# Startup mask, clock fillers and last copy of a block-sparse attention with a gated MLP behind it: one-hots by Pool selects, band by VectorE, row-tile fillers, split copy

## The chip, the cores and the metric

The kernel runs on one core of a Trainium2 chip. The metric is the device time of one execution in microseconds (us), given as the median over runs. Engines are named as in the profile: PE is TensorE (PEld its weight loads), DVE is VectorE, ACT is ScalarE, POOL is GpSimd, SP is the engine that issues most DMAs.

## The reference

For 4 batches, 8 heads, 768 tokens and head size 64, the reference computes attention with a block mask (blocks of 32 tokens, 24 x 24 blocks), and then a gated MLP on the 512 concatenated columns.

```python
scores = (1/8) * q @ k.T                      # per batch and head, 768 x 768
mask  = |block_i - block_j| <= 1              # band
mask |= block_i in (0, 23) or block_j in (0, 23)
mask |= block_j in sampled_blocks[block_i]    # 3 random blocks per row
x = softmax(where(mask, scores, -1e9)) @ v    # heads side by side: 4 x 768 x 512

h = relu(x @ w_in)                            # 512 -> 1024
u, v = h[..., :512], h[..., 512:]
v = (v - mean(v)) / sqrt(var(v) + 1e-6)       # per token
v = w_spatial @ v + b_spatial[:, None]        # over the 768 tokens
out = (u * v) @ w_out                         # 4 x 768 x 512, float32
```

## The kernel before

The mask is added inside the score matmul. Each head's transposed k (`kt`) and q (`qt`) tiles have 88 partitions: 64 of head data and 24 mask rows. In `kt`, mask row b holds a one at the tokens of block b (the block one-hots). In `qt`, the mask rows hold, per query token, 0 for an allowed block and -300 for a forbidden one; they come from one small matmul pair `mq` (L252) of the 24 x 24 block mask `bm` with the one-hots. So the score matmuls L289 (two of 384 columns per 128 keys) give masked scores, and ScalarE's exponential (L293, scale 0.125) follows. `av` (L305) multiplies by v, with a ones column that gives the softmax sums; `norm` divides.

The order is written out by hand and each engine executes its own list in program order; the recording layer adds the semaphore waits. The main loop goes over 16 head pairs in 12 steps each. A step issues one score chunk, some preparation of the next pairs, `av` of seven steps earlier, and a share of the MLP of the previous batch. The MLP of the last batch runs after the loop, as the tail.

The startup, in program order, is what the change touches:

- SP and ACT issue the loads of `sampled_blocks` (`samp_i`), k, q and v.
- VectorE writes zeros into `warm`, `allowed`, `ind_nat` and `tiny` (L170 to L173); ScalarE loads its function table and runs an exponential on `tiny`.
- TensorE gets `keep_warm(8, 512)` (L183): eight matmuls of 512 columns on zeros, whose result `wps` nobody reads. They keep TensorE active until data arrive.
- Pool makes `colidx`, five selects on `allowed` (band and border rows, L190 and L193), one select on `ind_nat` (L195, the one-hots in natural token order), `ident` (the identity for transposes), the ones column of `vv`, and `mhalf`.
- VectorE sets the border columns of `allowed`, casts `samp_i` to `samp_f` (L207), adds the sampled blocks in three steps (L209), forms `bm` (L213) and casts the first q head `nat_q` (L109). ScalarE casts the first k head `nat_k` (L107) and copies `ind_nat` into `ind` in the chunked token order (L217).
- `tr_head` (L225): six transposes of k on TensorE (L228) and a VectorE copy into `kt[0]` (L220); a VectorE copy of `ind` into the mask rows (L248); two fillers; the `mq` pair; a ScalarE copy of `mq` into `qt[0]` (L223); six transposes of q and their copy; six fillers; then the loop.

In the tail, 24 matmul units take their PSUM bank from `moe_ps`, which goes round the tags `sc`, `av` and `moe` (two buffers each) in `tail_tags`. The tag `moe` is also used by the transposes `xtr` just before the tail and by `g_tr` in it. Each output chunk is copied from PSUM to `osb` alternately by ScalarE (L447) and VectorE (L449) and stored by a DMA (L450).

```python
        tail_tags.rotate(1)                       # L355: moe, av, sc, moe, ...
```

The softmax here doesn't subtract the row's maximum and nothing guards it: scores larger than these inputs give would overflow.

## Time and profile before

| | |
|---|---|
| median of 7 runs | 227.0 us (226.46 to 228.18) |
| profiled execution | 227.45 us |
| its span | 225.5 us, 5286 instructions |
| busy | PE 214.6 (95%), ACT 171.1 (76%), DVE 131.1 (58%), POOL 64.1 (28%) |
| first filler matmul, first score matmul, first exponential | 1.17, 7.66, 8.19 us |
| last VectorE copy | 221.81 us, 0.69 us long |

The span is the time from the first to the last instruction on the core. A busy TensorE counts matmuls from their issue to their modelled end, so matmuls that overlap in the pipeline are counted once and a busy TensorE need not be at its peak. In a timeline line the columns are start, length, engine, source line, operation, tile written <- tiles read, shapes, count; in brackets stands the idle time in front and what ended it. In the chain of waits the columns are start, length, and the work or wait.

### The profile page before, as it was taken

To read this page: it belongs to the slowest core of one execution; us is meant where nothing else is said; L and a number is where in the kernel's file an instruction comes from. 1 tells how busy PE (TensorE), PEld (TensorE's weight loads), DVE (VectorE), ACT (ScalarE), POOL (GpSimd) and SP (SyncE) were. 2 spreads that over 40 slices of the span, in tenths; PEclk is the share of its full clock that TensorE was granted. 3 is DMA by queue.
4 is the path that set the end of the run, shared out by engine and by line. 5 is a ranking of instruction groups with operands and counts; after the bars stand their busy time and mean duration, and the time that the engine had idled before them with its cause. 6 is when DMAs were issued, how large, how long until landed. Compare 5 with 4: busy or idle time off the path is not lost.

```text
span 225.5 us, 5286 instructions
## 1 busy us (share of the span) xinstructions
PE 214.6 (95%) x2119; PEld 130.7 (58%) x2148; DVE 131.1 (58%) x282; ACT 171.1 (76%) x245; POOL 64.1 (28%) x88
## 2 busy tenths in 40 slices
PE   7899999999999999999999999999999999999993
PEld 3467777766665555666656555666565555544551
DVE  5556445368993444379993534469983323675532
ACT  5699999997799676878898677877898666266351
POOL 5535770349493401210283101211240000012000
PEclk9999999999999999999999999999999999999999
DMA  6689979996996974999465565987050424610016
GB/s 203 216 291 380 384 270 317 373 116 78 268 252 123 287 102 124 224 349 283 169 110 207 107 97 157 285 282 200 0 105 3 81 49 83 230 52 0 0 50 234
DMA packets 56093, 40.27 MB, mean 179 GB/s; under 512 B 39300, under 2 KB 51588, under 8 KB 56068
## 3 DMA queue, kind: packets, MB, share of 16 engines
q1 hardware_dynamic: 55780, 39.53, 65.6%
q10 hardware_dynamic: 288, 0.39, 0.5%
q8 instruction: 17, 0.28, 0.5%
q14 instruction: 8, 0.07, 0.1%
HBM read 24.38 MB, written 6.29 MB: 136 GB/s over the span
## 4 chain that ended last, share of the span: by engine, by line
PE 74%; ACT 19%; DMA 2%; issue 2%; DVE 1%; ACTq 0%
PE ps L289 21%; ACT a_all L293 19%; PE ps_av L305 10%; PE ps_moe L424 10%; PE ps_moe L402 7%; PE ps_moe L379 7%; PE ps_moe L442 5%; PE ps_t L424 2%; DMA out_dram<-osb 2%; PE wps L180 2%; PE ps_t L379 2%; PE ps_t L442 2%; PE ps_t L402 1%; PE ps_sc L424 1%; PE ps L228 1%
## 5 line engine op out<-in xcount | busy, mean ns | idle before, releaser
L293 ACT ACTIVATE a_all<-ps 128x768 bf16<-128x768 f32 x192 | 143.0, 812 | 29.9 <-PE ps L289 29.6
L289 PE MATMUL ps<-qt,kt 88*128 88x384 bf16 x384 | 93.5, 324 | 4.1 <-ACT a_all L293 2.8
L305 PEld LDWEIGHTS <-a_all 128*128 128x128 bf16 x1152 | 60.3, 98 | 28.5
L305 PE MATMUL ps_av<-vv,a_all 128*128 128x65 bf16 x1152 | 67.6, 194 | 0.0
L289 PEld LDWEIGHTS <-kt 88*128 88x128 bf16 x384 | 28.9, 97 | 8.2 <-issue 5.2
L427 DVE SCALAR_TENSOR_TENSOR gn<-ps_moe,b_col,un 128x512 bf16<-128x512 f32 x18 | 13.5, 751 | 27.3 <-PE ps_moe L424 27.3
L112 POOL CAST vv<-st_v 128x768 bf16<-128x768 f32 x16 | 13.4, 839 | 51.7 <-PE ps_av L305 46.9
L424 PE MATMUL ps_moe<-vn,w_spt 128*128 128x512 bf16 x99 | 24.8, 378 | 0.5
L424 PEld LDWEIGHTS <-w_spt 128*128 128x128 bf16 x144 | 13.8, 97 | 14.3
L392 POOL TENSOR_SCALAR std<-mv 128x3 f32<-128x3 f32 x8 | 1.9, 242 | 65.2 <-DVE mv L389 53.9
L109 POOL CAST nat_k<-st_k 128x768 bf16<-128x768 f32 x15 | 12.5, 833 | 21.5 <-DMA st_k<-in_k_dram 9.2
L319 DVE TENSOR_TENSOR xn<-ps_av,rc 128x384 bf16<-128x384 f32 x32 | 17.8, 557 | 1.1
L442 PE MATMUL ps_moe<-w_out_t,gt 128*128 128x512 bf16 x66 | 18.2, 378 | 0.3
L379 PE MATMUL ps_moe<-w_in_t,xt 128*128 128x512 bf16 x66 | 18.0, 378 | 0.3
L402 PE MATMUL ps_moe<-w_in_t,xt 128*128 128x512 bf16 x66 | 17.7, 378 | 0.3
L388 DVE BATCH_NORM_STATS2 stats<-vsb 128x6 f32<-128x512 bf16 x24 | 16.7, 694 | 1.9 <-ACT vsb L383 1.3
L379 PEld LDWEIGHTS <-xt 128*128 128x128 bf16 x96 | 9.3, 96 | 10.0 <-issue 0.7
L449 DVE COPY osb<-ps_moe 128x512 f32<-128x512 f32 x9 | 6.2, 691 | 15.0 <-PE ps_moe L442 14.9
L402 PEld LDWEIGHTS <-xt 128*128 128x128 bf16 x96 | 9.3, 96 | 9.6
L442 PEld LDWEIGHTS <-gt 128*128 128x128 bf16 x96 | 8.9, 97 | 8.4
L385 DVE TENSOR_SCALAR vsb<-ps_moe 128x512 bf16<-128x512 f32 x18 | 12.3, 681 | 1.5 <-PE ps_moe L379 1.4
L318 DVE RECIPROCAL rc<-ps_av 128x6 f32<-128x6 f32 x32 | 6.0, 187 | 12.2 <-PE ps_av L305 12.1
(82 smaller groups left out, 200.2 us busy)
## 6 DMA issues: line engine op xcount, KB each, us to landing
st_v<-in_v_dram SPq DMA_DIRECT2D x16, 384.0 KB, 5.4
out_dram<-osb SPq DMA_DIRECT2D x24, 256.0 KB, 2.5
st_q<-in_q_dram SPq DMA_DIRECT2D x15, 384.0 KB, 3.9
st_k<-in_k_dram SPq DMA_DIRECT2D x15, 384.0 KB, 4.8
wst<-in_moe_w_spatial_dram SPq DMA_DIRECT2D x3, 768.0 KB, 8.9
wst<-in_moe_w_in_dram SPq DMA_DIRECT2D x4, 512.0 KB, 9.3
wst<-in_moe_w_out_dram SPq DMA_DIRECT2D x2, 512.0 KB, 6.7
st_k<-in_k_dram ACTq DMA_DIRECT2D x2, 192.0 KB, 2.9
```

Source lines behind the costliest of these rows:

```text
L109: eng.tensor_copy(out=dst, in_=src)
L112: nc.gpsimd.tensor_copy(out=vv[p % 3][:, :, :, 0:D], in_=st.pop(("v", p)).rearrange("p h (c d) -> p h c d", d=D))
L289: nc.tensor.matmul(out=ps[:, hf * 512:hf * 512 + HALF], lhsT=kt[j % 4][:, ci * 128:(ci + 1) * 128], rhs=qt[j % 4][:, hf * HALF:(hf + 1) * ...
L293: nc.scalar.activation(out=a_ref[j][:, ci, :].rearrange("p (b c) -> p b c", b=2), in_=ps.rearrange("p (b c) -> p b c", b=2)[:, :, 0:HALF], ...
L305: nc.tensor.matmul(out=av_ref[j][:, qc, :], lhsT=a_ref[j][:, ci, qc * 128:(qc + 1) * 128], rhs=vv[p % 3][:, h, ci, :], start=(ci == 0), st ...
L319: nc.vector.tensor_tensor(out=xn_ref[p][:, :, h, :], in0=ps[:, :, 0:D], in1=rc.to_broadcast([128, NCH, D]), op=ALU.mult)
L379: nc.tensor.matmul(out=ps, lhsT=xt(g)[:, tcc * 128:(tcc + 1) * 128], rhs=w_in_t[:, g, DH:DFF], start=(g == 0), stop=(g == NDM - 1))
L388: nc.vector.bn_stats(out=stats, in_=vsb[:, tcc, :])
L402: nc.tensor.matmul(out=ps, lhsT=xt(g)[:, tcc * 128:(tcc + 1) * 128], rhs=w_in_t[:, g, 0:DH], start=(g == 0), stop=(g == NDM - 1))
L424: nc.tensor.matmul(out=ps, lhsT=w_spt[:, sc, tcc * 128:(tcc + 1) * 128], rhs=vn[:, sc, :], start=(sc == 0), stop=(sc == NCH - 1))
L427: nc.vector.scalar_tensor_tensor(out=gn[:, tcc, :], in0=ps, scalar=b_col[:, tcc:tcc + 1], in1=un[:, tcc, :], op0=ALU.add, op1=ALU.mult)
L442: nc.tensor.matmul(out=ps, lhsT=gt[:, tcc, dhc, :], rhs=w_out_t[:, dhc, :], start=(dhc == 0), stop=(dhc == NDH - 1))
```

## The change

Four parts.

1. *Mask rows in place.* `ind` is now the mask rows of `kt[0]` itself (partitions 64 to 87) and all small mask tiles lie on the same partitions. VectorE fills the rows with ones and Pool cuts them to the one-hots with two selects in the chunked token order. The tile `ind_nat`, ScalarE's copy L217 and VectorE's copy L248 go. The `mq` pair works on partitions 64 to 87.
2. *Band by VectorE.* The five Pool selects on `allowed` go. Pool makes three index tiles, and VectorE forms border rows and band with four small steps. VectorE writes the zeros of `ident`, ScalarE casts the first q head.
3. *Fillers.* Eight fillers of 512 columns become two of 512 columns, twelve of 65 columns, and 24 of 65 columns that use 64 rows each, alternately the upper and the lower half, into two PSUM banks. The two fillers of 128 columns in front of `mq` go.
4. *Tail.* `tail_tags` goes round in the order `sc`, `moe`, `av`; the last output chunk is copied by ScalarE and VectorE, half each.

```diff
-    nc.vector.memset(warm, 0.0)
-    nc.vector.memset(allowed, 0.0)
-    nc.vector.memset(ind_nat, 0.0)
-    nc.vector.memset(tiny, 0.0)
+    ind = kt[0][D:KR, :]
+    # allowed, colidx, dist, row, samp_i, samp_f, bm, sq: tiles on partitions D to KR too
+    nc.vector.memset(tiny, 0.0)
+    nc.vector.memset(warm, 0.0)
+    nc.vector.memset(ind, 1.0)
+    nc.vector.memset(ident, 0.0)
...
-    keep_warm(8, 512)
+    keep_warm(2, 512)
+    keep_warm(12, VA)
+    for _ in range(12):
+        for half, ps in ((0, wps), (1, wps2)):
+            rows = slice(64 * half, 64 * half + 64)
+            nc.tensor.matmul(out=ps[:, 0:VA], lhsT=warm[rows, 0:128], rhs=warm[rows, 0:VA],
+                             start=True, stop=True)
...
-    nc.gpsimd.iota(colidx, ...)
-    (five affine_selects on allowed, one on ind_nat, make_identity)
+    for t, pat, base, mul in ((colidx, 1, 0, 0), (dist, 1, 0, -1), (row, 0, 1 - NB, 2)):
+        nc.gpsimd.iota(t, pattern=[[pat, NB]], base=base, channel_multiplier=mul, ...)
+    tok = ind.rearrange("b (c p) -> b c p", c=NCH)
+    nc.gpsimd.affine_select(out=tok, in_=tok, compare_op=ALU.is_ge, fill=0.0, base=0,
+                            pattern=[[1, NCH], [NCH, 128]], channel_multiplier=-BLK)
+    nc.gpsimd.affine_select(out=tok, in_=tok, compare_op=ALU.is_ge, fill=0.0, base=BLK - 1,
+                            pattern=[[-1, NCH], [-NCH, 128]], channel_multiplier=BLK)
+    nc.gpsimd.affine_select(out=ident, in_=ident, compare_op=ALU.not_equal, fill=1.0, ...)
...
+    nc.vector.scalar_tensor_tensor(out=sq, in0=row, scalar=1.0, in1=row, mult, mult)
+    nc.vector.tensor_scalar(out=allowed, in0=sq, scalar1=float((NB - 1) ** 2), is_ge)
+    nc.vector.scalar_tensor_tensor(out=sq, in0=dist, scalar=1.0, in1=dist, mult, mult)
+    nc.vector.scalar_tensor_tensor(out=allowed, in0=sq, scalar=1.0, in1=allowed, is_le, max)
...
-    cast_qk(0, "q", slice(0, 1), nc.vector)
     cast_qk(0, "k", slice(0, 1), nc.scalar)
-    nc.scalar.activation(out=ind, in_=ind_nat.rearrange("b (p c) -> b c p", c=NCH), func=AF.Copy)
+    cast_qk(0, "q", slice(0, 1), nc.scalar)
...
     tr_head(0, "k", dve_copy)
-    nc.vector.tensor_copy(out=kt[0][D:KR, :], in_=ind)
-    keep_warm(2, 128)
     (the mq pair and its copy: partitions D to KR instead of 0 to NB)
...
-    tail_tags = deque(["sc", "av", "moe"])
-        tail_tags.rotate(1)
+    tail_tags = deque(["av", "sc", "moe"])
+        tail_tags.rotate(-1)
...
-                if tcc % 2 == 0:
+                if last and tcc == NCH - 1:
+                    nc.scalar.activation(out=osb[:, 0:DM // 2], in_=ps[:, 0:DM // 2],
+                                         func=AF.Copy)
+                    nc.vector.tensor_copy(out=osb[:, DM // 2:DM], in_=ps[:, DM // 2:DM])
+                elif tcc % 2 == 0:
```

## The prediction

> **What bounds the kernel now.** I read the chain of waits first, then the start and the end as timelines, because the change touches only these two.

> ```profile
> 1.17 3.59 PE wps L180 x8
> 4.77 0.78 PE ps L228 x6
> 5.54 0.33 PE wps L180 x2
> 5.87 0.68 PE mq L252 x2
> 6.56 0.47 PE ps L228 x6
> ...
> 7.05 0.56 DVE qt L220
> ...
> 7.66 0.51 PE ps L289 x2
> ```

> This is the chain up to the first score matmul, all TensorE in program order: eight fillers, six k transposes, two fillers, the two mask matmuls `mq`, six q transposes; then one VectorE copy releases L289 at 7.66. From 12.27 the chain is ScalarE's exponentials, later TensorE, and no input load stands in it. So I take a shift of the first score matmul to reach the end in full.

> ```profile
> 2.43 0.99 POOL L195 TENSOR_SCALAR_AFFINE_SELECT ind_nat<-ind_nat 24x768 bf16<-24x768 bf16 x1
> 3.63 0.29 POOL masks.py:199 TENSOR_SCALAR_AFFINE_SELECT ident<-ident 128x128 bf16<-128x128 bf16 x1
> 2.51 1.07 DVE L207 CAST samp_f<-samp_i 24x6 f32<-24x6 int32 x1 [0.96 <-DMA samp_i<-in_sampled_blocks_dram]
> 3.62 0.33 DVE L209 SCALAR_TENSOR_TENSOR allowed<-colidx,samp_f,allowed 24x24 f32<-24x24 f32 x1
> 4.52 0.17 DVE L213 TENSOR_SCALAR bm<-allowed 24x24 bf16<-24x24 f32 x1
> ```

> Pool and VectorE in the same stretch. A cast of six columns takes 1.07 us and ends at 3.59, when Pool's select and the memset behind it are done; the L209 step that began 0.01 us before Pool's 3.63 select ended 0.03 us after it, at 3.95. The next two L209 steps, with no select beside them, take 0.23 each, 0.265 start to start. So VectorE is held through Pool's selects. `bm` is ready at 4.69, and `mq` does not wait for it: TensorE only gets there at 5.80.

> ```profile
> 4.70 0.85 PE L228 MATMUL ps<-ident,nat_k 128*64 128x128 bf16 x6
> 5.80 0.75 PE L252 MATMUL mq<-ind,bm 24*24 24x384 bf16 x2
> 6.49 0.52 PE L228 MATMUL ps<-ident,nat_q 128*64 128x128 bf16 x6
> 7.66 0.50 PE L289 MATMUL ps<-qt,kt 88*128 88x384 bf16 x2 [0.20 <-DVE qt L220]
> ```

> The same six transposes take 0.85 us at 4.70 and 0.52 at 6.49, and two 384-column matmuls 0.75 and then 0.50: TensorE runs at half speed until about 6.4 us, 5.2 us after its first filler, and in those 5.2 us it paused about 0.4 in all. After the last matmul (221.79) the granted clock stays at 1.00 until 224.80 and is 0.52 over 224.80:225.54: it follows activity with a delay of some us.

> ```profile
> 196.22 0.70 DVE osb L449
> 196.97 1.24 PE ps_t L379 x5
> ...
> 221.79 0.02 issue
> 221.81 0.69 DVE osb L449
> ```

> At the start of the tail TensorE waits until VectorE has emptied the bank that the first tail unit takes over; the span ends with one VectorE copy of 0.69 and the output transfer.

> The profiled execution took 227.45 (span 225.5 plus 1.95 around it). The median of the seven runs is 227.0, 0.45 lower, and they spread from 226.46 to 228.18. About 0.3% (0.7 us) is what a measurement can tell from no change.

> **Pool's chain.** VectorE now writes `ident` and the 24x768 ones first. Zeros went as 256 uint32 in 0.27 and 384 in 0.38, 0.83 ns each above 0.06 fixed; the built instruction has 768 elements: 0.70 if it goes one by one, 0.38 if in pairs. I take 0.70, the slope of the rows. [...] After `tiny` and `warm` the ones end at 1.08+0.70=1.78, the first select starts at 1.84 and takes 0.99 (L195's row), the second 2.90 to 3.89 (0.07 between dependent Pool steps, as at 3.563 to 3.633), the `ident` select 3.96 to 4.25. Before, `ident` was ready at 3.93. So the five small selects (0.20 each), the memset and the 1.21 us ScalarE copy of `ind` that go were not on the path, and two selects of 0.99 in place of one are.

> **VectorE's chain.** New are four 24x24 steps, each waiting for the one before, with the cast, three L209 steps and `bm` queued behind them. As in the 3.62 row, a step that starts within some hundredths of a Pool select loses: the first square ends with the first select (2.86), the next step with the second (3.91), the second square with the `ident` select (4.28). Then the fourth step (0.23, the L209 row) from 4.31 to 4.54, two memsets (0.06), the cast to about 4.67 (0.1, below the 0.17 row, with no Pool beside it), three steps from 4.70 to 5.47 (2x0.265+0.23), `bm` from 5.50 to 5.67. `mq` can start at 5.71. If nothing were held, `bm` would be there before 4 and `mq` would follow the k transposes (below); if the cast too were caught by Pool's small memsets, 5.8. Ends: 5.1 to 5.8.

> **TensorE.** Two 512-column fillers from 1.20 at 0.427 (the spacing of eight in 3.59) end at 2.05. No row shows a cold 65-column matmul; a warm av matmul of that shape starts every 0.03, and 65 columns at the fillers' 0.83 ns are 0.054: twelve take 0.65. The 24 row tiles take 0.65 if their pairs overlap, 1.3 if not, 2.6 if each costs a cold 128-column step (0.107). I take 1.3, nearest to the shape's own rows: the fillers end near 4.1 with 0.14 for the switch (the pause in front of 4.70), just before `ident`. k transposes go from about 4.35 to 5.0; then TensorE, with the two fillers removed, idles until `mq` at 5.71. Before, `mq` began at 5.80: a gain of 0.1, with the q transposes, the copies and the first scores shifting alike. The q cast moved to ScalarE (0.52 after 3.73 or the landing) is ready before 5.2 and hides behind this wait, the removed 0.35 `ind` copy was hidden behind the q transposes, the remaining copies keep their places.

> **The clock.** This is the cost that I think decides. Over the 3.5 us from the fifth filler (1.17+4x0.427=2.88) to the rise at about 6.4, TensorE paused 0.4 us (three pauses of 0.14). In the same stretch it now works 1.2 (fillers) + 0.65 (k transposes) + 0.66 (`mq`) and pauses about 1.0, or 1.7 if the row tiles overlap. The 1.7 us of unbroken work before 2.88 had not brought full speed, and 3.1 in the stretch behind did; 1.8 to 2.5 lies at the lower end between. If it is too little, the rise comes later by as long as the clock takes to react, some 3 us by the fall at the end. [...] Cost of a rise near 9.5: the q transposes take 0.33 more (0.85 against 0.52), the first scores 0.25 more (0.75 against 0.50), and one or two exponentials wait on a cold step of 0.85 (two 384-column matmuls 0.64, two fillers 0.21, at the fillers' 0.83 ns) instead of the 0.70 between exponentials (four in 2.92 from 8.19, the last 0.81 long): 0.2. Sum 0.78, less 0.1 from `mq`: +0.7.

> **The end.** The first tail unit moves from the bank that VectorE empties until 196.91 to one long free. Its first three matmuls can follow the transposes at 196.55, its fourth waits for `xt`, copied by VectorE until 197.38, and starts near 197.43 instead of 197.61: gain 0.18, after which TensorE runs without a wait on the banks. The split copy: in the built program VectorE's half waits for ScalarE's half, as both read one bank. ScalarE's 512 columns take 0.60 and 768 take 0.81, so 256 take 0.39; VectorE's 0.69 for 512 less 256 at 1.04 ns is 0.43; with 0.03 between, 0.85 against 0.69: a loss of 0.16. Together -0.02; at the ends -0.18 and +0.16.

> **The cases.** *Late clock*: 227.45+0.7-0.02 = 228.1 for the profiled run, 227.7 carried to the median. I take 228.0: in a run whose clock comes early (the fast ones) the old chain is all TensorE and shrinks, while the new one is held at 5.71 by Pool and VectorE, so such runs lose 0.3 more. For it: the idle TensorE in front of `mq`. Chance 0.50.

> *Clock in time* (not slower beyond measurement): 227.45-0.1-0.02 = 227.3, 226.9 to 227.3 at the median. It decides if 1.8 to 2.5 us of work in those 3.5 is enough. Against it: 1.7 was not. Chance 0.25.

> *VectorE free, clock no later* (faster): selects and steps interleave, `mq` follows the k transposes at 5.1, 0.7 earlier, of which 0.3 is lost again if the q transposes run cold: 227.45-0.4-0.02 = 227.0, 226.6 at the median, and 226.2 if the many small matmuls bring the clock up sooner. For it: VectorE's steps are tiny; against it: the 1.07 us cast. Chance 0.15.

> *Fillers too long* (slower, or the change not doing what it says): row tiles at 0.107 end at 5.4, the k transposes at 6.1, `mq` at 6.3: +0.5, 227.9, 227.5 at the median. Chance 0.10.

> **Numbers.** 228.0. Slower by over 0.3%: most of the first case and half of the last, 0.55. Faster: the third and a little of the second, 0.17. Within: 0.28. Low end 226.4 with most of the third case; high end 228.9, the first with the `mq` end of 5.8 (0.1), the split's 0.16 alone and a clock another 0.6 later.

> **What would show it.** Right: Pool's second 24x768 select ending near 3.9 with VectorE steps of about 1 us beside it, `bm` near 5.67, TensorE idle for 0.6 us in front of `mq`, q transposes of 0.8 instead of 0.52, the last VectorE half starting where ScalarE's half ends. Wrong: `bm` before 5, or q transposes at 0.52 and the first score matmul before 7.4, or halves side by side.

## The result and the profile after

The changed kernel takes 228.69 us (median of 12 runs, 228.08 to 229.88); the kernel before took 227.08 us beside it (31 runs, 226.46 to 228.28). The ratio is 1.007, with a 95% interval of 1.0053 to 1.0088: 1.6 us slower. Ratios, here and below, leave out runs more than 1.5% above the fastest of the same kernel. The profiled execution took 228.8 us, its span 227.1.

The chain of waits of the changed kernel, from the start (columns: start, length, work):

```profile
1.43 0.70 DVE kt L180
2.35 0.76 DVE sq L215
3.34 0.73 DVE sq L219
...
5.73 0.81 PE mq L267 x2
6.54 0.78 PE ps L245 x6
...
10.71 0.64 PE ps L304 x2
11.56 0.78 PE ps L245 x6
...
12.96 0.45 PE ps L245 x6
```

Up to 5.73 the chain is VectorE, where it was TensorE before. But `mq` (L267) starts at 5.73, 0.07 earlier than before. The loss comes behind it. Six transposes take 0.78 at 6.54 and still 0.78 at 11.56, then 0.45 at 12.96; a score pair takes 0.64 still at 10.71. TensorE runs at half speed (called cold below: 512 columns every 0.427 us in the first fillers, every 0.215 in the tail) for twice as long as before. The trace's record of the granted clock has the rise at 12.46 us; in the kernel before it stands at 6.37.

VectorE and Pool over the mask (timeline of each engine):

```profile
2.35 0.75 DVE L215 SCALAR_TENSOR_TENSOR sq<-row 24x24 f32<-24x24 f32 x1
3.13 0.17 DVE L217 TENSOR_SCALAR allowed<-sq 24x24 f32<-24x24 f32 x1
3.34 0.72 DVE L219 SCALAR_TENSOR_TENSOR sq<-dist 24x24 f32<-24x24 f32 x1
4.09 0.17 DVE L221 SCALAR_TENSOR_TENSOR allowed<-sq,allowed 24x24 f32<-24x24 f32 x1
...
5.51 0.17 DVE L231 TENSOR_SCALAR bm<-allowed 24x24 bf16<-24x24 f32 x1
```

```profile
2.20 0.86 POOL L204 TENSOR_SCALAR_AFFINE_SELECT kt<-kt 24x768 bf16<-24x768 bf16 x1 [0.97 <-DVE kt L180]
3.13 0.89 POOL L206 TENSOR_SCALAR_AFFINE_SELECT kt<-kt 24x768 bf16<-24x768 bf16 x1
4.09 0.34 POOL L208 TENSOR_SCALAR_AFFINE_SELECT ident<-ident 128x128 bf16<-128x128 bf16 x1
```

The two squares L215 and L219, 24x24 each, take 0.75 and 0.72 and end about 0.03 behind the selects beside them (3.10 behind 3.07, 4.06 behind 4.03). L217 between them takes 0.17 although a select runs beside it, and so does L221 beside the `ident` select; in the trace both start 0.001 before their select, the two squares 0.15 and 0.20 behind theirs. `bm` is ready at 5.68.

TensorE in the same stretch (its timeline):

```profile
2.90 0.84 PE L197 MATMUL wps<-warm 64*128 64x65 bf16 x24
4.48 0.80 PE L245 MATMUL ps<-ident,nat_k 128*64 128x128 bf16 x6 [0.74 <-POOL ident L208]
5.73 0.81 PE L267 MATMUL mq<-kt,bm 24*24 24x384 bf16 x2 [0.45 <-DVE bm L231]
6.47 0.85 PE L245 MATMUL ps<-ident,nat_q 128*64 128x128 bf16 x6
7.96 0.82 PE L304 MATMUL ps<-qt,kt 88*128 88x384 bf16 x2
```

The row tiles run two side by side, a pair every 0.0545 us (the two of a pair start within 0.003 of each other), and are issued in 0.65. TensorE then waits 0.74 for `ident` and 0.45 for `bm` (both counted from the modelled end of its work). Of the two rows that answer to those of before, the q transposes take 0.85 instead of 0.52, and the first score pair starts at 7.96 instead of 7.66 and takes 0.82 instead of 0.50.

How this adds up, in the start times of the exponentials against the profiled execution of before: the first is 0.63 late, the next three 0.78, 0.94 and 1.10, the fifth 1.61, and from there to the last of the 192 it stays at 1.61. Each of the three steps costs 0.155 because a cold score pair with two fillers needs 0.85 (0.64 and 0.21) where the exponentials come 0.70 apart; the fifth has the cold k transposes in front of it as well.

The end, from the chain of waits:

```profile
223.26 0.39 ACT osb L462
...
223.68 0.42 DVE osb L464
```

VectorE's half starts at 223.68, when ScalarE's half is done (223.65). Counted from the start of the last `x` transpose (L343; L328 before), the first tail matmul starts after 0.056 us (before 0.475), the fourth after 0.939 (1.120), the last of all after 24.739 (24.907), and the last copy ends after 25.996 (26.015). Up to the last copy the tail is even to 0.02.

### The profile page after: what moved, and what is told of

It is laid out like the page before. It is cut to its first block, busy times and chain, and to the rows that moved or that the text cites. A ratio compares the mean times of both kernels' runs of the same rounds, so it can differ in the third digit from the quotient of the medians.

```text
span 227.1 us, 5340 instructions
## 1 busy us (share of the span) xinstructions
PE 215.6 (95%) x2147; PEld 132.6 (58%) x2176; DVE 131.6 (58%) x284; ACT 171.2 (75%) x246; POOL 64.0 (28%) x85
## 4 chain that ended last, share of the span: by engine, by line
PE 77%; ACT 17%; DVE 3%; issue 2%
PE ps L304 23%; ACT a_all L308 17%; PE ps_av L320 11%; PE ps_moe L439 10%; PE ps_moe L394 7%; PE ps_moe L457 7%; PE ps_moe L417 7%; PE ps_t L439 2%; PE ps_t L457 2%; PE ps_t L394 2%; PE ps_t L417 1%; PE ps_sc L439 1%; PE ps L245 1%; PE ps_sc L417 1%; PE ps_sc L457 1%
## 5 line engine op out<-in xcount | busy, mean ns | idle before, releaser
L304 PE MATMUL ps<-qt,kt 88*128 88x384 bf16 x384 | 95.0, 328 | 3.5 <-ACT a_all L308 2.5
L421 DVE TENSOR_SCALAR vn<-vsb,mv,rstd 128x512 bf16<-128x512 bf16 x24 | 12.7, 564 | 0.6 <-POOL rstd L409 0.5
```

What stands on the lines that cost most here:

```text
L304: nc.tensor.matmul(out=ps[:, hf * 512:hf * 512 + HALF], lhsT=kt[j % 4][:, ci * 128:(ci + 1) * 128], rhs=qt[j % 4][:, hf * HALF:(hf + 1) * ...
L421: nc.vector.tensor_scalar(out=vn[:, tcc, :], in0=vsb[:, tcc, :], scalar1=mv[:, tcc, 0:1], scalar2=rstd[:, tcc:tcc + 1], op0=ALU.subtract, ...
```

## The experiments

Two theories stood at the outset. *Clock*: the new fillers and TensorE's pauses put off the rise of the clock, and nothing else matters. Rival, *mask chain*: the time goes where VectorE and Pool now hold back `mq`. Each ratio below is against runs of the kernel before that were made with it; their medians were 226.8 to 227.0.

**1. The changed kernel with the old fillers.** Only the fillers go back.

```diff
-    keep_warm(2, 512)
-    keep_warm(12, VA)
-    (24 row tiles)
+    keep_warm(8, 512)
...
+    keep_warm(2, 128)            # in front of mq
```

> The changed kernel with the fillers of before (eight of 512 columns, two of 128 in front of the mask matmuls); mask chain and tail stay changed. Theory clock: the k transposes start at 4.7 and mq at 5.8 as before, full speed comes at the same phases as before, so all of the loss goes: 227.1 (ratio to before 1.000, give or take 0.001). Rival mask chain: the loss lies in Pool's two long selects and VectorE's held steps, which are still there, so it stays at 228.3 to 228.7.

Measured: 227.1 (226.85 to 228.3) against 226.99, ratio 1.0009 [0.9984, 1.0033]. The chain of waits:

```profile
4.87 0.71 PE ps L238 x6
5.58 0.22 PE wps L188 x2
5.80 0.43 PE mq L261 x2
6.22 0.47 PE ps L238 x6
```

`bm` is ready at 5.68 as in the changed kernel, and `mq` follows the two fillers without a wait, by the timeline at 5.73 in both. Yet `mq` takes 0.43 and the q transposes 0.47: the clock rose at 5.38. So the loss is in the fillers; what the new mask and the tail cost together cannot be told from nothing (the interval is -0.4 to +0.7 us).

**2. The kernel before with the new fillers.** The reverse, with none in front of `mq`.

```diff
-    keep_warm(8, 512)
+    keep_warm(2, 512)
+    keep_warm(12, VA)
+    (24 row tiles)
...
-    keep_warm(2, 128)            # in front of mq
```

> The kernel before with the new fillers alone (two of 512, twelve of 65, 24 row tiles of 65, none in front of mq); mask chain and tail as before. Theory clock: the k transposes start 0.7 earlier (4.0) and mq at 4.9 to 5.0, but full speed comes one to two steps of 3.4 us later, first score matmul near 7.2, and the time is 228.0 to 228.6. Rival mask chain: without the slower mask chain the shorter fillers are a pure gain, 226.5.

Measured: seven of twelve runs lie between 226.16 and 229.05, with a median of 227.8; their ratio, 1.0023 [0.999, 1.0057], is not clear of no change. The other five (229.6 to 230.0) are not in it. The profiled execution took 228.3:

```profile
5.81 0.78 PE ps L235 x6
...
10.83 0.78 PE ps L235 x6
...
12.30 0.45 PE ps L235 x6
```

Its first exponential is 0.10 earlier than before, but the clock rises at 11.88 and from the fifth exponential on it is 0.95 late. In this execution the fillers alone put off the rise; what they cost in the median this experiment does not show.

**3. The changed kernel with the pauses filled.** Eight fillers more, 0.85 us of work.

```diff
     (24 row tiles)
+    keep_warm(5, 128)
...
+    keep_warm(3, 128)            # in front of mq
```

> The changed kernel with 0.85 us of fillers more, put where TensorE idled: five of 128 columns behind the row tiles (ending at 4.3, before the k transposes at 4.48) and three in front of mq (ending at 5.6, mq still at 5.73). Theory clock by idle time: full speed comes a step sooner in most runs, 227.3 to 227.8. Rival, that the clock follows how much of the array the matmuls use (row tiles, 64-column transposes and 24-row mq count little): not much better, 228.2 to 228.6. Rival mask chain: unchanged, 228.7.

Measured: 227.03 (226.84 to 229.3), ratio 1.0012 [0.9983, 1.0041]; seven of twelve runs lie between 226.84 and 227.09. 0.85 us more of fillers brings 1.66 us back, with `mq` still at 5.73. So the pauses, not the mask chain behind them, were the loss. The profiled execution was one of the exceptions (229.3), for a reason of its own that the chain of waits and the busy time by stretches show (in the second, per stretch: PE, PEld, DVE, ACT and POOL busy, then the granted clock):

```profile
17.47 0.84 POOL nat_k L108
```

```profile
15.00:19.20 4.20, 2.75 (x37) 1.84 (x37) 1.69 (x5) 2.79 (x5) 1.73 (x3) 0.99 0.90 282
19.20:22.50 3.30, 3.30 (x31) 2.28 (x29) 1.56 (x3) 2.42 (x3) 2.72 (x3) 0.50 1.05 397
```

Pool's cast of a later k block began at 17.47 (15.29 before), after its load, which landed at 17.32 (15.14 before), and TensorE had to wait for it. TensorE worked 2.75 of the 4.20 us from 15.00 on, and from 19.14 to 22.55 the clock was down to 0.50. This execution's rise at the start, 5.48, was early all the same.

**4. The tail order alone.** The kernel before with the new order of banks.

```diff
-    tail_tags = deque(["sc", "av", "moe"])
+    tail_tags = deque(["av", "sc", "moe"])
...
-        tail_tags.rotate(1)
+        tail_tags.rotate(-1)
```

> The kernel before with the new bank order of the tail alone, for its profile. Prediction's step: the first tail matmul follows the last transpose by 0.06 us, the fourth waits for xt, and from the last transpose to the end of the last matmul it takes 0.18 less than before (25.07 before, from 196.55 to 221.79 less the 0.17 of modelled end; 24.89 expected). Rival, that another bank becomes late further on: no gain.

One execution, 228.0. Its startup is that of before to the instruction, and still its clock rose at 9.95 and not at 6.37. Counted from the last `x` transpose, the last copy ends after 25.848 instead of 26.015: the order gains 0.167. The split copy of the changed kernel, which ends at 25.996, gives 0.148 of that back.

**5 and 6. Half the columns, half the rows.** What does the clock look at? The old fillers of the kernel before, with 64 of 128 weight columns, and with 64 of 128 rows (the partitions that the operands use); both stream the same 512 columns in the same time.

```diff
-    keep_warm(8, 512)
+    for _ in range(8):           # half_cols: wps[0:64], warm[:, 0:64] x warm[:, 0:512]
+        nc.tensor.matmul(...)    # half_rows: wps, warm[0:64, 0:128] x warm[0:64, 0:512]
```

> The kernel before with its eight first fillers using half of the array's columns (64 of 128 weight columns, all 128 rows, still 512 moving columns, so TensorE is busy for the same time). Theory array use (rows times columns times time decides the clock; in the profiles so far it rose after stretches of 3.41 us with 0.63 or more and stayed low at 0.58 or less): the fillers count half, the rise comes one step or two later in most runs, q transposes and first scores cold, 228.0 to 228.8. Theory busy time: unchanged, 227.1. Theory rows (only the used rows count): unchanged, 227.1.

> The kernel before with its eight first fillers using half of the array's rows (partitions 0 to 63 alone, all 128 columns, 512 moving columns, same time). Theory array use and theory rows: the rise comes late as in half_cols, 228.0 to 228.8. Theory busy time, or that only used columns count: unchanged, 227.1.

Half the columns: 226.9 (226.34 to 228.18), ratio 0.9987 [0.9964, 1.0009]. Half the rows: 228.9 (228.25 to 229.12), ratio 1.0072 [1.0048, 1.0095], all of the change's loss with none of its edits. The chain of waits with half the rows:

```profile
1.17 3.59 PE wps L184 x8
...
5.87 0.74 PE mq L254 x2
6.61 0.78 PE ps L230 x6
...
11.62 0.78 PE ps L230 x6
```

The fillers last 3.59 as before and `mq` starts at 5.87 as before, so TensorE is as busy as before; but the clock rises at 12.39. With half the columns it rises at 4.28, and the k transposes are fast already (timeline):

```profile
1.17 3.43 PE L184 MATMUL wps<-warm 128*64 128x512 bf16 x8 [1.17 <-DVE allowed L171]
4.44 0.50 PE L230 MATMUL ps<-ident,nat_k 128*64 128x128 bf16 x6
```

That led to a count, which was worked out from the profiles of this case alone. In the records of the granted clock the full speed lasts 218.453 us before (6.37 to 224.83) and 215.040 after (12.46 to 227.50): 64 and 63 times 3.413. In experiment 3 the clock was down for one such time (19.14 to 22.55), and its fall came four of them after its rise at 5.48. Cut the time into such stretches, ending at the rise. In each, add up for every matmul its share of the 128 rows times the time that its columns stream (0.83 ns each while cold, from the fillers' 0.427 for 512), and divide by 3.413:

| kernel | row share of the stretches up to the rise | rise at, us |
|---|---|---|
| before | 0.53, 0.75 | 6.37 |
| after | 0.28, 0.54, 0.65, 0.75 | 12.46 |
| 1 old fillers | 0.21, 0.96 | 5.38 |
| 2 new fillers | 0.15, 0.67, 0.68, 0.75 | 11.88 |
| 3 pauses filled | 0.24, 0.82 | 5.48 |
| 4 tail order | 0.58, 0.71, 0.80 | 9.95 |
| 5 half the columns | 0.91 | 4.28 |
| 6 half the rows | 0.15, 0.57, 0.66, 0.75 | 12.39 |
| 7 tail in two banks | 0.97 | 4.45 |
| 8 six fillers | 0.47, 0.68, 0.81 | 9.58 |
| 9 full rows in `mq` | 0.55, 0.82 | 6.46 |
| 10 no row tiles | 0.21, 0.61, 0.60, 0.77 | 12.19 |

In all twelve the clock rose at the end of the first stretch with 0.75 or more (the lowest, after and kernel 6, hold 0.748), and never after one of 0.71 or less. The same sums without the rows do not sort them: by streamed time alone a stretch of 0.92 (half the rows, 2.15 to 5.56) brought no rise and one of 0.89 (before, 2.96 to 6.37) did; by rows times columns, 0.46 did (half the columns) and 0.58 did not (tail order, 3.12 to 6.54). The transposes count: without them the rise of kernel 9 would rest on 0.44, while 0.49 (kernel 2, 5.06 to 8.47, counted likewise) brought none. Rows counted in groups of 32 (24 as 32, 88 as 96) would sort the twelve as well, 0.76 and more against 0.72 and less; no run tells the two counts apart.

**7. A tail in two banks.** The kernel before with the new order, and with the last chunk computed as two halves of 256 columns in two banks, so that the copies need not wait for each other.

```diff
+                halves = 2 if last and tcc == NCH - 1 else 1
+                for hf in range(halves):     # own bank, own 4 matmuls of DM // halves columns
+                    (VectorE copies the first half, ScalarE the second)
```

> The kernel before, startup untouched, with the changed bank order of the tail and with the last output chunk computed as two halves of 256 columns in two banks: VectorE copies the first while TensorE makes the second, ScalarE copies the second. Theory bank (the halves wait for each other because they share a bank): from the last transpose of x to the last output DMA 25.55 to 25.6 instead of 26.04 (0.17 from the order, 0.3 from the copy), 226.6 in all (ratio 0.998). Rival, that the second copy or the DMA waits for something else: 26.0 and 227.1.

Measured: 226.39 (226.06 to 227.74), ratio 0.9983 [0.9963, 1.0004]. The chain of waits:

```profile
220.67 0.44 DVE osb L450
221.10 0.38 ACT osb L452
```

VectorE copies its half while TensorE works on the other. ScalarE's half starts as VectorE's ends, but also as its own last matmul ends (221.07); its wait for VectorE had been met by 220.34, before VectorE's copy began, so here the halves did not wait for each other. The last copy ends 25.548 after the last `x` transpose, 0.47 earlier than before. With run to run differences in the rise of the clock on top, the ratio alone does not prove it; the intervals in the trace do.

**8. Fewer fillers.** Kernel 7 with two fillers fewer, so that the k transposes start as soon as `ident` is there.

```diff
-    keep_warm(8, 512)
+    keep_warm(6, 512)
...
-    keep_warm(6, 128)            # behind the q transposes
+    keep_warm(8, 128)
```

> tail_two_banks with six first fillers of 512 columns instead of eight, and eight instead of six of 128 behind the q transposes. Theory clock by array use: k transposes at 4.0 and mq at 5.1, 0.7 earlier, but the rise comes a step late in a third to a half of the runs: two groups, near 226.2 and near 227.5, median 226.3 to 227.0, spread wider than tail_two_banks. Rival, that the fillers only cost time: 225.9 to 226.1 throughout.

Measured: 227.12, in two groups: five runs from 225.78 to 226.03, seven from 227.11 to 227.34; ratio 0.998 [0.9956, 1.0003]. The profiled execution is of the upper group and missed its rise with a stretch of 0.68. A startup this short seems to reach the 0.75 of the table or not, depending on where the stretches lie; kernel 9 tests this.

**9. Full rows in `mq`.** Kernel 8 with the 24-row operands of `mq` padded with zeros to 128 rows: same time, more rows.

```diff
-        nc.tensor.matmul(out=mq[0:NB, ...], lhsT=bm, rhs=ind[:, ...], start=True, stop=True)
+        nc.tensor.matmul(out=mq[0:NB, ...], lhsT=bm_all, rhs=ind_all[:, ...], start=True, stop=True)
```

> The kernel six_fillers with one thing more: the operands of the mask product mq are padded with zero rows from 24 to 128, so that each of its matmuls feeds all 128 rows and takes the time that it took. Theory (the clock rises after a stretch of the 3.41 us grid in which the rows in use, as a share of 128, times the time streamed are 0.75 or more, and not at 0.71 or less): in six_fillers the runs lay in two groups, 225.8 to 226.0 and 227.1 to 227.3, because for some positions of the grid the best stretch held 0.68; mq at full rows adds up to 0.76 x 104/128 = 0.6 us, that is 0.18 of a stretch, so the upper group vanishes: 225.8 to 226.1 in all fast runs, ratio 0.995 to 0.996. Rival (what divides the two groups is no matter of rows): two groups as before, near 225.9 and 227.2, ratio 0.997 to 0.999. Second rival (the memory fills that the padding needs delay the mask on VectorE or GpSimd): all runs 0.3 to 0.6 above the lower group, 226.2 to 226.6.

Measured: 225.62 (seven runs, 225.44 to 226.19) against 226.8 (226.35 to 228.35), ratio 0.9934 [0.9905, 0.9964], a little below the forecast. The upper group is gone. The timeline of TensorE:

```profile
5.04 0.82 PE L256 MATMUL mq<-ind_all,bm_all 128*24 128x384 bf16 x2
5.78 0.83 PE L232 MATMUL ps<-ident,nat_q 128*64 128x128 bf16 x6
7.26 0.50 PE L293 MATMUL ps<-qt,kt 88*128 88x384 bf16 x2
```

`mq` starts 0.76 earlier than before, and the clock rises at 6.46, in time for the scores; the first exponential is 0.40 earlier. (Another 0.31 came between 30 and 43 us, where in the kernel before one exponential had waited 0.23 for L305; the cause is open.) This version beats both kernels: 1.2 us under the one before, 3.1 under the changed one. It keeps the mask of before and takes from the change only the order of the tail.

**10. No row tiles.** The changed kernel with twelve 65-column fillers of 128 rows in place of the 24 of 64.

```diff
-    (24 row tiles)
+    keep_warm(12, VA)
```

> The changed kernel with its 24 row tiles (64 rows each, two side by side) replaced by twelve matmuls of full 128 rows and 65 columns, which take the same 0.65 us. Theory (rows in use count; two tiles of 64 rows side by side are worth one of 128): nothing changes, 228.7, ratio 1.006 to 1.008, clock rise near 12.4 us. Rival (the form of the row tiles is what keeps the clock down): the rise comes a stretch or two earlier and the time falls to 227.1 to 227.7, ratio 1.000 to 1.003.

Measured: 228.73 (227.98 to 230.73), ratio 1.0064 [1.0034, 1.0094], rise at 12.19. The form of the row tiles is not to blame: with one of 128 rows in place of two of 64 side by side, the rise (12.46 with the tiles) and the time (228.69) stayed where they were, to 0.27 and 0.04. What the change lost is the time in which fillers stream: 8 x 0.427 = 3.42 us before, 2 x 0.427 + 2 x 0.65 = 2.15 after, besides 0.21 in front of `mq`.

## Why the prediction was right, and where it was not

The forecast of 228.0 (226.4 to 228.9) with the late clock as the likeliest case held: 228.69, though the loss was 1.6 and not 1.0. Step by step:

- **Pool's chain, right.** The ones took 0.70 as worked out from the slope, not 0.38. Two sizes were off and partly cancelled: the ones began at 1.43 and not at 1.08, and the two selects took 0.86 and 0.89, not 0.99, so that the second ended at 4.03 and not at 3.89.
- **VectorE held by Pool, right in the sum, in part by luck.** `bm` was forecast for 5.67 and came at 5.68; `mq` for 5.71 and came at 5.73. The rule taken from the 3.62 row, that a step which starts within some hundredths of a select loses, failed twice: L217 was to be held until the second select ended and took 0.17 beside it, and L221 took 0.17 beside the `ident` select. So the second square ended with the second select instead of the `ident` select, 0.22 early; the cast, put at 0.1, took 0.34 and made up for it. The order of the starts (the held L215 and L219 0.15 and 0.20 behind their select, L217 and L221 0.001 ahead of theirs) sorts these four, though not the 3.62 row, which began 0.01 ahead and was held. What decides stays open.
- **TensorE, right by cancellation.** I took 1.3 us for the row tiles; they were issued in 0.65, the other case that I named. It changed nothing for `mq`, as the k transposes had to wait for `ident` anyway, which came at 4.43 and not at 4.25.
- **The clock, right in kind, too small in size: the term that failed.** "A rise near 9.5" was 3.1 us, about one stretch, later than before. It came 6.09 later, nearly two stretches, at 12.46. Of the terms, the q transposes were put at +0.33 and measured +0.33; the first scores at +0.25, measured +0.32; `mq` at -0.1, measured -0.02 by the start of the q transposes; but "one or two exponentials on a cold step: 0.2" became four steps worth 0.98 (1.61 - 0.63). With that term the sum of the steps is the measured 1.6.
- **The reason given for it was wrong.** I counted TensorE's working time in the 3.5 us up to the rise. Experiments 5, 6 and 9 show that rows count: by the table's count `mq`, with 24 rows, is worth a fifth of its time, and the stretch that ended at 9.05 held 0.89 of streaming but 0.65 in rows. In these runs busy time without rows did not decide: 0.92 of streaming with half the rows brought no rise, and 0.89 in the kernel before did.
- **Run to run.** Where the stretches lie differs between executions. Experiment 4 had the startup of before, a stretch from 3.12 to 6.54 with 0.71 where before had one from 2.96 to 6.37 with 0.75, and its rise at 9.95 instead of 6.37. The group at 228.15 to 228.3 among the runs of before fits this (228.0 and the 0.167 of the order); no profile shows one of these runs.
- **Why it was not worse.** In the cold loop a score pair of 88 rows (0.64) and two fillers (0.21) give 0.75 to 0.77 in rows. In the four profiles that came that far cold (after, kernels 2, 6 and 10) the first stretch that lies wholly in the loop brought the rise, and the loss ended there. A stretch of 0.71 (experiment 4) brought no rise, so with 0.75 to 0.77 it need not be so in every run. In my terms, the range's "clock another 0.6 later" stood for this. The term was off by 0.78; that 228.69 still fell inside the range is in part luck, as the 0.1 and 0.16 that the high end also held did not come.
- **The 0.3 added for runs with an early clock, not seen.** No run shows this term: the lowest moved by 1.62 (226.46 to 228.08) and the highest by 1.60 (228.28 to 229.88). That the clock comes earlier in some runs than in others was my assumption then; of the same startup, experiment 4 later showed a rise at 9.95 beside the 6.37 of before.
- **The tail, right.** Order -0.18 forecast, -0.167 measured; split +0.16 forecast, +0.148 measured; together -0.02 in both. VectorE's half took 0.425 (0.43 forecast) where the whole chunk takes 0.691 before: 1.04 ns for each of the 256 columns less, as I had put it.

Of the rivals, *clock in time* failed on the rows (0.65 in the stretch that ended at 9.05), *VectorE free* on the held squares (0.75 and 0.72), and *fillers too long* on the pairs running side by side (0.0545 each).

## What to carry to other kernels

In these profiles, a startup that has to bring TensorE to full speed is to be read as rows times streamed time in each 3.41 us stretch, not as busy or idle. Work with few rows, such as the 24-row mask product, can be padded to all 128 with zeros (`mq` took 0.82 padded and 0.81 not, both cold), and a filler is removed only if the 0.75 in rows, behind which the clock rose in all twelve, is still there wherever the stretches happen to lie. And a copy split over two engines paid (0.30 us) when each half had a bank of its own and the first half was computed first; in one bank it cost 0.15.
